# Linear attention and MLP mixer on one core: VectorE subtracts the float32 pairs' maxima, and the tiles stand in three pools

## The chip, the cores and the metric

One NeuronCore of a Trainium2 chip runs the whole program. The metric is the device time of one execution in microseconds (us), the median of the runs. A profile of one execution comes with it: a trace of every instruction on the engines TensorE (PE, its weight loads PEld), VectorE (DVE), ScalarE (ACT), GpSimd (POOL) and the DMA queues, most of them issued from SP.

## The reference

Eight sequences of 576 tokens, eight heads of 64. Attention with an exponential feature map, then a token mixer and a channel mixer:

```python
def phi(x):
    proj = np.einsum('bhsd,df->bhsf', x, w_phi)                      # 128 features
    proj = proj - np.max(np.abs(proj), axis=-1, keepdims=True)
    return np.concatenate([np.exp(proj), np.exp(-proj)], axis=-1)
q_p, k_p = phi(q), phi(k)
kv = np.einsum('bhsf,bhsd->bhfd', k_p, v);  z = np.sum(k_p, axis=2)
x = einsum('bhsf,bhfd->bhsd', q_p, kv) / (einsum('bhsf,bhf->bhs', q_p, z)[..., None] + 1e-06)
# x: heads side by side, [8, 576, 512]
u  = x + (np.maximum(x.T @ w_tok1, 0) @ w_tok2).T                     # tokens 576 -> 256 -> 576
out = u + np.maximum(u @ w_ch1, 0) @ w_ch2                            # channels 512 -> 1536 -> 512
```

The four mixer weights come as 64-bit floats.

## The kernel before

Heads are taken in 32 pairs, four for each batch element. Nearly every product is made of float32r operands split in a high and a low part, three matmuls each (`mm3`, L77 to L82). Pairs 0 to 3 (`i < PLAIN`), the four of batch 0, skip the split: their projections, keys and queries are plain float32. They are what "float32 pairs" means.

Five Python generators are written out in turn by `weave`: `keys` (projection ppk, maximum mxk, exponentials kp, product pkv with v into kv), `queries` (projection ppq and its tail ppt, maximum, difference pm, transposition pt, exponentials qf, split into qh and ql, product pn, division by den into xt), `token_stream` (per batch two halves of 256 channels: px transposes xt, xh and xl are its parts, pa the first product, ah and al the hidden values' parts, ph the second product, added into xt), `load_weights` (24 blocks of the channel weights and seven of the token weights), and `channel_stream` (18 pieces of 256 tokens: uh and ul are the parts of xt, h the up product, gh and gl its parts, acc the down product). A scheduler that simulates the engines' time then sets the order on each engine; each engine takes its instructions in that order, and waits at each for what it needs.

A group of projections is 128 rows by one or two times 128 features, in PSUM. `less_max` takes the absolute maximum over the features on VectorE (L226). In the pairs from 4 on, GpSimd subtracts it (L237) and ScalarE takes the two exponentials, one of each sign (L282). In pairs 0 to 3 GpSimd only negates the maximum (nmx, L229). Keys' exponentials are then four ScalarE instructions of 128 features straight from PSUM, with the maximum or its negative as bias (L285); queries' differences are one ScalarE instruction for each 128 features, with the negative as bias (L235).

A block of weights is converted by ScalarE (L131), four VectorE instructions on the tile `bits` (L132 to L135), and then split by ScalarE (L72) and GpSimd (L75).

Tiles stand in two SBUF pools: `cst` for what stays and `wk` for what turns over. What TensorE streams, and some weights, are made by `streamed`: a tile with 32 spare elements, used from the 16th on. `column` pads the maxima to 32 elements. `eps` takes 40 elements for one.

Of the kernel before, what the change touches and what calls it, by code (L numbers as in the profile page):

```python
# [42 lines left out]
def mixer_kernel(ctx, tc, qk, vm, vt, w_phi, w1, w2, wc1, wc2d, out):  # L43
    nc = tc.nc

    cst = ctx.enter_context(tc.tile_pool(name="cst", bufs=1))
# [8 lines left out]
    def streamed(pool, shape, dtype, **kw):

        n = 1
        for k in shape[1:]:
            n *= k
        t = pool.tile([P, n + 32], dtype, **kw)[:, 16:16 + n]  # L60
        if len(shape) == 3:
            t = t.rearrange("p (a b) -> p a b", a=shape[1])
        return t

    def column(pool, n, **kw):

        return pool.tile([P, 32], F32, **kw)[:, :n]

# [20 lines left out]
    wp2 = streamed(cst, [P, 2, F], F32R, name="wp2")  # L89
    wp = cst.tile([P, F], F32, name="wp")  # L90
# [13 lines left out]
    for j in range(2):  # L104
        t = cst.tile([P, 672], F32, name=f"v{j}")[:, :650].rearrange("p (u j d) -> p u j d", u=5, j=2)
        nc.gpsimd.memset(t[:, 4], 0.0)
        nc.gpsimd.memset(t[:, 0:4, :, D:], 1.0)
        for i in range(2):
            nc.gpsimd.memset(t[i * D:(i + 1) * D, 4, i, D:], 1.0)
# [81 lines left out]
    def less_max(ts, units, name, base=None):  # L191
# [25 lines left out]
        if base is None:  # L217
            part = wk.tile([P, 2, F], F32, tag="part", name=f"part{name}")
            nc.scalar.copy(part[:, :n], ps[:, :n, 1])
# [1 line left out]
            nc.vector.tensor_tensor(pr[:, :n], ps[:, :n, 0], part[:, :n], op=ALU.add)
# [4 lines left out]
        nc.vector.tensor_reduce(mx[:, :n], pr, axis=AX.X, op=ALU.max, apply_absolute_value=True)  # L226
        if base is not None:
            nmx = column(wk, 2, tag="nmx", name=f"nmx{name}")
            nc.gpsimd.tensor_scalar(nmx[:, :n], mx[:, :n], -1.0, None, op0=ALU.mult)  # L229
        if base == D:  # L230
            return pr, nmx, mx
        pm = wk.tile([P, 2, F], F32, tag=f"pm{kind}", name=f"pm{name}", bufs=1 if kind == "t" else 2)
        if base == 0:
            for i in range(n):
                nc.scalar.activation(pm[:, i], pr[:, i], AF.Identity, bias=nmx[:, i:i + 1])  # L235
        else:
            nc.gpsimd.tensor_tensor(pm[:, :n], pr, mx[:, :n].unsqueeze(2).to_broadcast([P, n, F]), op=ALU.subtract)  # L237
        return pm
# [23 lines left out]
    def keys():  # L262
        groups = [[(0, 0), (0, 1)], [(0, 2), (0, 3)], [(1, 0), (1, 1)], [(1, 2), (1, 3)], [None]]
        todo = None
        for i in range(B * NP):
# [11 lines left out]
            for g, us in enumerate(groups):  # L277
                pm = less_max(ts, us, f"k{i}_{g}", plain)
                kp = wk.tile([P, 2, 2, F], F32, tag="kp", name=f"kp{i}_{g}")
                for sg in range(2):  # L280
                    if i >= PLAIN:
                        nc.scalar.activation(kp[:, :len(us), sg], pm[:, :len(us)], AF.Exp, scale=1.0 - 2.0 * sg)  # L282
                        continue
                    for n in range(len(us)):
                        nc.scalar.activation(kp[:, n, sg], pm[0][:, n], AF.Exp, bias=pm[1 + sg][:, n:n + 1],  # L285
                                             scale=1.0 - 2.0 * sg)
# [70 lines left out]
    def turn(i, k, j, pm, tail):  # L357
# [11 lines left out]
        for sg in range(2):  # L369
            full = wk.tile([P, SEG[0][1]], F32, tag="qf", name=f"qf{i}_{k}{j}{sg}")[:, :w]  # L370
# [7 lines left out]
            (nc.gpsimd if sg else nc.vector).tensor_tensor(lo, full, hi.bitcast(F32), op=ALU.subtract)  # L378
# [92 lines left out]
    def channel_mix(i, segs):  # L471
        uh, ul = [], []
        for c in range(NC_):
            h = streamed(wk, [P, CH], F32R, tag=f"uh{c}", name=f"uh{i}_{c}", bufs=1)
# [144 lines left out]
```

## Time and profile before

| | us |
|---|---|
| median of 3 runs | 1182.55 (1182.36 to 1184.48) |
| the profiled execution's own time | 1180.86 |
| its span in the trace | 1178.9 |
| TensorE busy | 1134.0 |
| VectorE busy | 702.9 |
| ScalarE busy | 673.5 |
| GpSimd busy | 584.8 |

A row of the profile's groups reads: line, engine, operation, tiles written and read, shapes, count, then busy us, mean ns of one, idle time of the engine before them and what ended it. The forty slices give busy tenths. Rows by stage give for each stretch the busy us and count of PE, PEld, VectorE, ScalarE and GpSimd, then the clock granted to TensorE, the share of the DMA engines and GB/s. A row of the timeline gives start, duration, engine, line and operation.

### The profile page before, as it was taken

How to read it: one execution, taken by the hardware profiler on the slowest of the kernel's cores; microseconds unless marked ns; L12 is line 12 of the kernel's file. 1: busy time of each engine (PE TensorE's matmuls, PEld its weight loads, DVE VectorE, ACT ScalarE, POOL GpSimd, SP SyncE). 2: the span in 40 equal slices, each digit the busy share in tenths (PEclk: the TensorE clock that was granted, in tenths of full speed). 3: DMA queues.
4: the chain of work that ended last, by engine and by line, in shares of the span. 5: the costliest groups of instructions: out<-in, count | busy, mean ns of one | idle time of the engine just before them, and what ended most of it. 6: DMA issues, size and time to landing. Idle time of an engine off the chain costs nothing.

```text
span 1178.9 us, 24080 instructions
## 1 busy us (share of the span) xinstructions
PE 1134.0 (96%) x9032; PEld 1099.9 (93%) x9032; DVE 702.9 (60%) x1406; ACT 673.5 (57%) x1913; POOL 584.8 (50%) x774
## 2 busy tenths in 40 slices
PE   8877999999999999999999999999999999999998
PEld 6655889998999999998999999999999989999998
DVE  6899783566746666657656565474665666553111
ACT  6988784575746565566646455563665666441110
POOL 3567783465636564565546355462554655430000
PEclk9877799999999999999999999999999999999999
DMA  9543120111101111111111011110111110000000
GB/s 232 177 142 113 31 78 2 49 32 49 31 19 38 42 31 40 41 40 41 31 48 33 19 32 49 31 50 7 43 32 49 40 40 11 19 1 19 19 19 18
DMA packets 65299, 54.30 MB, mean 46 GB/s; under 512 B 44768, under 2 KB 56416, under 8 KB 65184
## 3 DMA queue, kind: packets, MB, share of 16 engines
q1 hardware_dynamic: 63824, 52.41, 15.4%
q8 instruction: 71, 1.16, 0.4%
q10 hardware_dynamic: 1360, 0.36, 0.1%
q14 instruction: 44, 0.36, 0.1%
HBM read 43.32 MB, written 9.44 MB: 45 GB/s over the span
## 4 chain that ended last, share of the span: by engine, by line
PE 84%; DVE 6%; ACT 6%; issue 2%; POOL 1%; DMA 1%; SPq 0%; POOLq 0%; DVEq 0%; ACTq 0%
PE acc L81 26%; PE h L81 26%; PE pkv L308 8%; PE pn L81 7%; PE ph L81 4%; PE pa L81 3%; PE pt L364 2%; PE ppk L212 2%; PE ppq L212 2%; DVE bitsc L135 1%; DVE bitsc L134 1%; PE px L432 1%; DVE bitsc L132 1%; ACT kp L285 1%; DVE den L410 1%
## 5 line engine op out<-in xcount | busy, mean ns | idle before, releaser
L81 PE MATMUL acc<-gh,wc 128*128 128x256 f32 x1728 | 339.7, 283 | 0.1
L81 PEld LDWEIGHTS acc<-gh,wc 128*128 128x128 f32 x1728 | 274.4, 188 | 0.4 <-ACT gh L498 0.4
L81 PE MATMUL h<-ul,wc_h 128*128 128x256 f32 x864 | 245.4, 284 | 1.9 <-POOL ul L479 1.8
L81 PE MATMUL h<-uh,wc_h 128*128 128x256 f32 x864 | 245.7, 285 | 0.5 <-DVE gl L499 0.5
L81 PE MATMUL h<-uh,wc_l 128*128 128x256 f32 x864 | 244.2, 283 | 0.0
L81 PE MATMUL acc<-gl,wc 128*128 128x256 f32 x864 | 243.2, 284 | 0.0
L308 PE MATMUL pkv<-v,kp 128*128 128x65 f32 (+1 forms) x1152 | 166.7, 280 | 6.9 <-ACT kp L285 4.3
L378 POOL TENSOR_TENSOR ql<-qf,qh 128x320 fp32r<-128x320 f32 (+1 forms) x112 | 93.0, 830 | 160.2 <-ACT qh L377 160.0
L308 PEld LDWEIGHTS pkv<-v,kp 128*128 128x128 f32 x1152 | 157.1, 202 | 14.6 <-ACT kp L285 7.9
L81 PEld LDWEIGHTS h<-ul,wc_h 128*128 128x128 f32 x864 | 162.8, 188 | 3.1 <-POOL ul L479 3.1
L81 PEld LDWEIGHTS h<-uh,wc_h 128*128 128x128 f32 x864 | 162.4, 188 | 1.1 <-DVE gl L499 1.1
L81 PEld LDWEIGHTS h<-uh,wc_l 128*128 128x128 f32 x864 | 163.2, 189 | 0.0
L81 PEld LDWEIGHTS acc<-gl,wc 128*128 128x128 f32 x864 | 162.9, 188 | 0.0
L499 DVE SCALAR_TENSOR_TENSOR gl<-h,gh 128x512 fp32r<-128x512 f32 x108 | 74.0, 685 | 144.1 <-ACT gh L498 143.1
L371 ACT ACTIVATE qf<-pt 128x320 f32<-128x320 f32 (+1 forms) x256 | 105.5, 416 | 85.9 <-PE pt L364 84.6
L282 ACT ACTIVATE kp<-pmk 128x256 f32<-128x256 f32 x280 | 96.0, 392 | 72.7 <-POOL pmk L237 69.6
L498 ACT ACTIVATE gh<-h 128x512 fp32r<-128x512 f32 x108 | 64.5, 598 | 112.8 <-PE h L81 112.1
L410 DVE RECIPROCAL den<-den 128x320 f32<-128x320 f32 x64 | 124.7, 1949 | 3.7 <-ACT den L406 2.3
L81 PE MATMUL pn<-qh,kv 128*128 128x320 f32 (+1 forms) x448 | 114.8, 297 | 0.6 <-ACT qh L377 0.3
L378 DVE TENSOR_TENSOR ql<-qf,qh 128x320 fp32r<-128x320 f32 (+1 forms) x112 | 70.1, 626 | 58.1 <-ACT qh L377 57.7
L237 POOL TENSOR_TENSOR pmk<-pk,mxk 128x256 f32<-128x256 f32 (+1 forms) x140 | 86.0, 614 | 35.7 <-DVE mxk L226 35.4
L187 POOL TENSOR_TENSOR stq<-raw,stq 64x512 fp32r<-64x512 f32 (+1 forms) x56 | 80.2, 1433 | 43.5 <-ACT stq L186 36.7
(112 smaller groups left out, 2418.4 us busy)
## 6 DMA issues: line engine op xcount, KB each, us to landing
raw<-in_qk SPq DMA_DIRECT2D x27, 576.0 KB, 3.8
rawc<-in_wc SPq DMA_DIRECT2D x24, 512.0 KB, 3.8
v<-in_vm SPq DMA_DIRECT2D x31, 256.0 KB, 3.4
out_x<-xt SPq DMA_DIRECT2D x12, 256.0 KB, 2.2
out_x<-xt SPq DMA_DIRECT2D x16, 192.0 KB, 2.0
raw<-in_w SPq DMA_DIRECT2D x8, 256.0 KB, 4.1
out_x<-xt SPq DMA_DIRECT2D x16, 128.0 KB, 1.9
pair<-in_qk SPq DMA_DIRECT2D x8, 160.0 KB, 4.5
```

Of the source, the lines that this page charges most:

```text
L81: nc.tensor.matmul(o, a, m, start=first and i == 0, stop=last and i == 2, skip_group_check=group_ok)
L187: nc.gpsimd.tensor_tensor(t[lo:lo + D], src, t[base:base + D].bitcast(F32), op=ALU.subtract)
L212: nc.tensor.matmul(ps[:, i].rearrange("p two f -> p (two f)"), t[:, c:c + P], wp2.rearrange("p two f -> p (two f)"), start=True, stop=True)
L237: nc.gpsimd.tensor_tensor(pm[:, :n], pr, mx[:, :n].unsqueeze(2).to_broadcast([P, n, F]), op=ALU.subtract)
L282: nc.scalar.activation(kp[:, :len(us), sg], pm[:, :len(us)], AF.Exp, scale=1.0 - 2.0 * sg)
L308: nc.tensor.matmul(o, kp[:, n, sg], v, start=g == 0 and n == 0 and sg == 0, stop=u is None, skip_group_check=True)
L364: nc.tensor.transpose(ptr[:, n], r, ident)
L371: nc.scalar.activation(full, src, AF.Exp, scale=1.0 - 2.0 * sg)
L378: (nc.gpsimd if sg else nc.vector).tensor_tensor(lo, full, hi.bitcast(F32), op=ALU.subtract)
L410: nc.vector.reciprocal(den, den)
L498: nc.scalar.activation(gh, ph, AF.Relu)
L499: nc.vector.scalar_tensor_tensor(gl, ph, 0.0, gh.bitcast(F32), op0=ALU.max, op1=ALU.subtract)
```

## The change

In `less_max`, pairs 0 to 3 now do what the others do, with VectorE in GpSimd's place: VectorE subtracts the maxima from the projections in PSUM and writes pm to SBUF, in one instruction for a group of up to 256 columns. The negations go. ScalarE's exponentials of the keys are then one instruction for each sign, from SBUF and without a bias, and the queries' differences are no longer ScalarE's.

```diff
-            pr = pr[:, :n]
+            pr, eng = pr[:, :n], nc.gpsimd
         else:
-            pr = ps[:, :n, 0]
+            pr, eng = ps[:, :n, 0], nc.vector
-        mx = column(wk, 2, tag=f"mx{kind}", name=f"mx{name}")
+        mx = odd.tile([P, 2], F32, tag=f"mx{kind}", name=f"mx{name}")
         nc.vector.tensor_reduce(mx[:, :n], pr, axis=AX.X, op=ALU.max, apply_absolute_value=True)
-        if base is not None:
-            nmx = column(wk, 2, tag="nmx", name=f"nmx{name}")
-            nc.gpsimd.tensor_scalar(nmx[:, :n], mx[:, :n], -1.0, None, op0=ALU.mult)
-        if base == D:
-            return pr, nmx, mx
         pm = wk.tile([P, 2, F], F32, tag=f"pm{kind}", name=f"pm{name}", bufs=1 if kind == "t" else 2)
-        if base == 0:
-            for i in range(n):
-                nc.scalar.activation(pm[:, i], pr[:, i], AF.Identity, bias=nmx[:, i:i + 1])
-        else:
-            nc.gpsimd.tensor_tensor(pm[:, :n], pr, mx[:, :n].unsqueeze(2).to_broadcast([P, n, F]), op=ALU.subtract)
++        eng.tensor_tensor(pm[:, :n], pr, mx[:, :n].unsqueeze(2).to_broadcast([P, n, F]), op=ALU.subtract)
         return pm
...
                 for sg in range(2):
-                    if i >= PLAIN:
-                        nc.scalar.activation(kp[:, :len(us), sg], pm[:, :len(us)], AF.Exp, scale=1.0 - 2.0 * sg)
-                        continue
-                    for n in range(len(us)):
-                        nc.scalar.activation(kp[:, n, sg], pm[0][:, n], AF.Exp, bias=pm[1 + sg][:, n:n + 1],
-                                             scale=1.0 - 2.0 * sg)
+                    nc.scalar.activation(kp[:, :len(us), sg], pm[:, :len(us)], AF.Exp, scale=1.0 - 2.0 * sg)
```

The second part is where tiles stand. `streamed` and `column` go. A pool `st` holds the streamed tiles, without spare elements; a pool `odd` holds v, eps, qf, den and the maxima. Two unused tiles of 32 and 192 bytes stand first in `cst` and `st`:

```diff
+    st = ctx.enter_context(tc.tile_pool(name="st", bufs=2))
+    odd = ctx.enter_context(tc.tile_pool(name="odd", bufs=2))
+    cst.tile([P, 8], F32, name="lead")
+    st.tile([P, 48], F32, tag="lead", name="lead2", bufs=1)
...
-    eps = cst.tile([P, 40], F32, name="eps")[:, :1]
+    eps = odd.tile([P, 1], F32, tag="eps", name="eps", bufs=1)
...
-        t = cst.tile([P, 672], F32, name=f"v{j}")[:, :650].rearrange("p (u j d) -> p u j d", u=5, j=2)
+        t = odd.tile([P, 5, 2, D + 1], F32, tag=f"v{j}", name=f"v{j}", bufs=1)
...
-            h = streamed(wk, [P, CH], F32R, tag=f"uh{c}", name=f"uh{i}_{c}", bufs=1)
+            h = st.tile([P, CH], F32R, tag=f"uh{c}", name=f"uh{i}_{c}", bufs=1)
```

The order on the engines changes up to the 315th instruction of VectorE's 1448 and the 728th of TensorE's 8354; from there on it is the same as before.

VectorE at the program's start, before (mx are the maxima of pair 0's groups, wp_80 the split projection weights, bits a block of weights):

```order
L226 TENSOR_REDUCE mxk_0_114<-ppk_0_111 128x2
L74 CAST wp_80<-wp 128x128
L75 TENSOR_TENSOR wp_80<-wp,wp_80 128x128
L226 TENSOR_REDUCE mxk_1_155<-ppk_1_152 128x2
L226 TENSOR_REDUCE mxq_00_145<-ppq_00_142 128x2
L226 TENSOR_REDUCE mxt_125<-ppt_123 128x1
L132 TENSOR_SCALAR bits_0_134<-bits_0_134 128x512
```

VectorE at the same place in the changed kernel (its lines have other numbers: L218 is the reduction, L220 the subtraction):

```order
L218 TENSOR_REDUCE mxk_0_122<-ppk_0_119 128x2
L66 CAST wp_88<-wp 128x128
L220 TENSOR_TENSOR pmk_0_124<-ppk_0_119,mxk_0_122 128x256
L67 TENSOR_TENSOR wp_88<-wp,wp_88 128x128
L218 TENSOR_REDUCE mxk_1_156<-ppk_1_153 128x2
L220 TENSOR_TENSOR pmk_1_158<-ppk_1_153,mxk_1_156 128x256
L218 TENSOR_REDUCE mxq_00_149<-ppq_00_146 128x2
L220 TENSOR_TENSOR pmq_00_151<-ppq_00_146,mxq_00_149 128x256
```

Each reduction is followed by its subtraction, at once or a few rows on.

VectorE around the low part of the first hidden values of batch 0 (al_0), before (den_1 is pair 3's last reciprocal, bitsc_8 to bitsc_10 are channel weights):

```order
L134 SCALAR_TENSOR_TENSOR bitsc_10_2304<-rawc_10_2302,bitsc_10_2304 128x512
L410 RECIPROCAL den_1_1112<-den_1_1112 128x256
L135 SCALAR_TENSOR_TENSOR bitsc_9_2212<-rawc_9_2210,bitsc_9_2212 128x512
L135 SCALAR_TENSOR_TENSOR bitsc_10_2304<-rawc_10_2302,bitsc_10_2304 128x512
L75 TENSOR_TENSOR xl_0_4_1068<-px_0_4_1064,xh_0_4_1067 128x256
L221 TENSOR_TENSOR pk_4_1194<-ppk_4_1190,partk_4_1192 128x128
L226 TENSOR_REDUCE mxk_4_1196<-pk_4_1194 128x1
L458 SCALAR_TENSOR_TENSOR al_0_1119<-pa_0_962,ah_0_1118 128x512
L221 TENSOR_TENSOR pk_0_1223<-ppk_0_1218,partk_0_1221 128x256
```

VectorE around the same instruction (L436 now) in the changed kernel:

```order
L126 SCALAR_TENSOR_TENSOR bitsc_0_1024_1889<-rawc_0_1024_1887,bitsc_0_1024_1889 128x512
L218 TENSOR_REDUCE mxk_3_1065<-pk_3_1063 128x2
L125 TENSOR_SCALAR bitsc_1_1024_1951<-bitsc_1_1024_1951 128x512
L124 TENSOR_SCALAR bitsc_2_1024_2004<-bitsc_2_1024_2004 128x512
L127 SCALAR_TENSOR_TENSOR bitsc_0_1024_1889<-rawc_0_1024_1887,bitsc_0_1024_1889 128x512
L436 SCALAR_TENSOR_TENSOR al_0_1039<-pa_0_888,ah_0_1038 128x512
L213 TENSOR_TENSOR pk_4_1114<-ppk_4_1110,partk_4_1112 128x128
L126 SCALAR_TENSOR_TENSOR bitsc_1_1024_1951<-rawc_1_1024_1949,bitsc_1_1024_1951 128x512
L125 TENSOR_SCALAR bitsc_2_1024_2004<-bitsc_2_1024_2004 128x512
L218 TENSOR_REDUCE mxk_4_1116<-pk_4_1114 128x1
```

Before, 120 of the conversions' 124 VectorE instructions stand ahead of al_0; now 99 do. The blocks of the last third of wc1 and the last of wc2 have moved behind it.

TensorE around the last matmul of batch 0's token mixing (ph_1_1_1), before (pt and ppk belong to pairs 5 and 6):

```order
L81 MATMUL ph_1_0_1_1538<-w_h,al_1_1452 128x256
L364 MATMUL pt_01_1951<-ident,pmq_01_1869 128x128 x2
L81 MATMUL h_0_1655<-uh_2_1645,wc_h 128x256
L81 MATMUL ph_1_1_1_1577<-w_h,ah_1_1451 128x256
L81 MATMUL ph_1_1_1_1577<-w_l,ah_1_1451 128x256
L81 MATMUL ph_1_1_1_1577<-w_h,al_1_1452 128x256
L308 MATMUL pkv_1882<-v_92,kp_2_1948 128x65 x4
L212 MATMUL ppk_4_2166<-wp_80,stk_1692 128x256
```

TensorE at the same matmul in the changed kernel (pn_11 belongs to pair 4):

```order
L73 MATMUL ph_1_1_1_1497<-w_h,ah_1_1371 128x256
L73 MATMUL ph_1_1_1_1497<-w_l,ah_1_1371 128x256
L73 MATMUL ph_1_1_1_1497<-w_h,al_1_1372 128x256
L204 MATMUL ppq_00_1645<-wp_88,stq_1629 128x256 x2
L73 MATMUL h_0_1575<-uh_2_1565,wc_h 128x256
L73 MATMUL pn_11_1675<-qh_110_1537,kv_4_1181 128x256
L73 MATMUL pn_11_1675<-ql_110_1538,kv_4_1181 128x256
```

Before, the last of these ph matmuls is the 479th on TensorE; now it is the 442nd. The 37 that stood ahead of it and now stand behind belong to pairs 4 to 6.

More of the change, by code (lines that the diff above doesn't have):

```diff
@@ L53, in mixer_kernel @@
     REST = dict(tag="rest", bufs=3)
[L55 to L67, printed above, removed]
     def split(hi, lo, raw, eng_hi, eng_lo):
@@ L86, in mixer_kernel @@
     make_identity(nc, ident)
-    eps = cst.tile([P, 40], F32, name="eps")[:, :1]
+    eps = odd.tile([P, 1], F32, tag="eps", name="eps", bufs=1)
     nc.gpsimd.memset(eps, 1e-6)
-    wp2 = streamed(cst, [P, 2, F], F32R, name="wp2")
+    wp2 = st.tile([P, 2, F], F32R, tag="wp2", name="wp2", bufs=1)
     wp = cst.tile([P, F], F32, name="wp")
@@ L96, in mixer_kernel @@
     w1_l = cst.tile([P, 5, T], F32R, name="w1_l")
-    w2_h = streamed(cst, [P, NT, S], F32R, name="w2_h")
-    w2_l = streamed(cst, [P, NT, S], F32R, name="w2_l")
+    w2_h = st.tile([P, NT, S], F32R, tag="w2_h", name="w2_h", bufs=1)
+    w2_l = st.tile([P, NT, S], F32R, tag="w2_l", name="w2_l", bufs=1)
     wc1_h = cst.tile([P, NC_, E], F32R, name="wc1_h")
@@ L128, in convert @@
         top, low = raw[:, :, 1], raw[:, :, 0]
-        m = streamed(wk, [P, 512], U32, tag="bits", name=f"bits{name}", bufs=3)[:w, :n]
+        m = wk.tile([P, 512], U32, tag="bits", name=f"bits{name}", bufs=3)[:w, :n]
         nc.scalar.activation(m.bitcast(F32), top.bitcast(F32), AF.Abs)
@@ L221, in less_max @@
             nc.vector.tensor_tensor(pr[:, :n], ps[:, :n, 0], part[:, :n], op=ALU.add)
-            pr = pr[:, :n]
+            pr, eng = pr[:, :n], nc.gpsimd
         else:
-            pr = ps[:, :n, 0]
-        mx = column(wk, 2, tag=f"mx{kind}", name=f"mx{name}")
+            pr, eng = ps[:, :n, 0], nc.vector
+        mx = odd.tile([P, 2], F32, tag=f"mx{kind}", name=f"mx{name}")
         nc.vector.tensor_reduce(mx[:, :n], pr, axis=AX.X, op=ALU.max, apply_absolute_value=True)
-        if base is not None:
-            nmx = column(wk, 2, tag="nmx", name=f"nmx{name}")
-            nc.gpsimd.tensor_scalar(nmx[:, :n], mx[:, :n], -1.0, None, op0=ALU.mult)
-        if base == D:
-            return pr, nmx, mx
-        pm = wk.tile([P, 2, F], F32, tag=f"pm{kind}", name=f"pm{name}", bufs=1 if kind == "t" else 2)
-        if base == 0:
-            for i in range(n):
-                nc.scalar.activation(pm[:, i], pr[:, i], AF.Identity, bias=nmx[:, i:i + 1])
-        else:
-            nc.gpsimd.tensor_tensor(pm[:, :n], pr, mx[:, :n].unsqueeze(2).to_broadcast([P, n, F]), op=ALU.subtract)
+        pm = wk.tile([P, 2, F], F32, tag=f"pm{kind}", name=f"pm{name}", bufs=1 if kind == "t" else 2)
+        eng.tensor_tensor(pm[:, :n], pr, mx[:, :n].unsqueeze(2).to_broadcast([P, n, F]), op=ALU.subtract)
         return pm
@@ L369, in turn @@
         for sg in range(2):
-            full = wk.tile([P, SEG[0][1]], F32, tag="qf", name=f"qf{i}_{k}{j}{sg}")[:, :w]
+            full = odd.tile([P, SEG[0][1]], F32, tag="qf", name=f"qf{i}_{k}{j}{sg}")[:, :w]
             nc.scalar.activation(full, src, AF.Exp, scale=1.0 - 2.0 * sg)
@@ L374, in turn @@
                 continue
-            hi = streamed(wk, [P, SEG[0][1]], F32R, tag="qh", name=f"qh{i}_{k}{j}{sg}")[:, :w]
-            lo = streamed(wk, [P, SEG[0][1]], F32R, tag="ql", name=f"ql{i}_{k}{j}{sg}")[:, :w]
+            hi = st.tile([P, 384], F32R, tag="qh", name=f"qh{i}_{k}{j}{sg}")[:, :w]
+            lo = st.tile([P, 384], F32R, tag="ql", name=f"ql{i}_{k}{j}{sg}")[:, :w]
             nc.scalar.activation(hi, src, AF.Exp, scale=1.0 - 2.0 * sg)
@@ L391, in numerators @@
         if j == 0:
-            dens[0] = wk.tile([P, SEG[0][1]], F32, tag="den", name=f"den{i}_{k}", bufs=1)[:, :w]
+            dens[0] = odd.tile([P, SEG[0][1]], F32, tag="den", name=f"den{i}_{k}", bufs=1)[:, :w]
         den = dens[0]
@@ L433, in token_mix @@
             if w < P:
-                xs = streamed(wk, [P, 2, P], F32R, tag="xh", name=f"xs{b}_{h}")
+                xs = st.tile([P, 2, P], F32R, tag="xh", name=f"xs{b}_{h}")
                 nc.scalar.copy(xs[:w], px[:w])
@@ L445, in token_mix @@
                 continue
-            xh = streamed(wk, [P, 2, P], F32R, tag="xh", name=f"xh{b}_{h}_{u}")[:w]
-            xl = streamed(wk, [P, 2, P], F32R, tag="xl", name=f"xl{b}_{h}_{u}")[:w]
+            xh = st.tile([P, 2, P], F32R, tag="xh", name=f"xh{b}_{h}_{u}")[:w]
+            xl = st.tile([P, 2, P], F32R, tag="xl", name=f"xl{b}_{h}_{u}")[:w]
             split(xh, xl, px[:w], nc.scalar, nc.vector)
@@ L473, in channel_mix @@
         for c in range(NC_):
-            h = streamed(wk, [P, CH], F32R, tag=f"uh{c}", name=f"uh{i}_{c}", bufs=1)
-            l = streamed(wk, [P, CH], F32R, tag=f"ul{c}", name=f"ul{i}_{c}", bufs=1)
+            h = st.tile([P, CH], F32R, tag=f"uh{c}", name=f"uh{i}_{c}", bufs=1)
+            l = st.tile([P, CH], F32R, tag=f"ul{c}", name=f"ul{i}_{c}", bufs=1)
             d = 0
@@ L495, in up_proj @@
                     mm3(ph[:, k], (wc1_h[:, c, es], wc1_l[:, c, es]), (uh[c], ul[c]), c == 0, c == NC_ - 1)
-            gh = streamed(wk, [P, 2, CH], F32R, tag="g", name=f"gh{i}_{ep}", bufs=4)
-            gl = streamed(wk, [P, 2, CH], F32R, tag="g", name=f"gl{i}_{ep}", bufs=4)
+            gh = st.tile([P, 2, CH], F32R, tag="g", name=f"gh{i}_{ep}", bufs=4)
+            gl = st.tile([P, 2, CH], F32R, tag="g", name=f"gl{i}_{ep}", bufs=4)
             nc.scalar.activation(gh, ph, AF.Relu)
```

## The prediction

> **What bounds the kernel now.** I read the page's busy table and the forty slices first, then the chain that ended last, then the busy time by stage, then the groups of instructions of the first stages.
>
> ```profile
> PE 1134.0 (96%) x9032; PEld 1099.9 (93%) x9032; DVE 702.9 (60%) x1406; ACT 673.5 (57%) x1913; POOL 584.8 (50%) x774
> PE   8877999999999999999999999999999999999998
> DVE  6899783566746666657656565474665666553111
> ACT  6988784575746565566646455563665666441110
> PEclk9877799999999999999999999999999999999999
> PE 84%; DVE 6%; ACT 6%; issue 2%; POOL 1%; DMA 1%; SPq 0%; POOLq 0%; DVEq 0%; ACTq 0%
> ```
>
> TensorE is full from the sixth slice on, and its clock reaches full speed there. Only the first four or five slices have VectorE and ScalarE as busy as that. The 6% and 6% that they hold of the chain come from there. The stages in numbers (busy us of PE, PEld, DVE, ACT, POOL with counts, then the granted clock, DMA share, GB/s):
>
> ```profile
> 0.00:10.00 10.00, 5.15 (x22) 4.69 (x22) 1.96 (x6) 3.24 (x8) 2.39 (x19) 1.00 0.81 220
> 10.00:42.00 32.00, 31.53 (x136) 25.22 (x138) 27.08 (x55) 27.32 (x81) 15.96 (x23) 0.84 0.81 213
> 42.00:131.00 89.00, 70.09 (x326) 54.16 (x324) 84.19 (x125) 71.80 (x191) 59.19 (x62) 0.76 0.41 124
> 131.00:167.00 36.00, 33.10 (x237) 30.19 (x237) 29.04 (x66) 31.87 (x92) 27.61 (x36) 0.97 0.18 53
> 167.00:191.00 24.00, 24.00 (x206) 24.00 (x206) 12.43 (x24) 14.55 (x40) 13.93 (x17) 1.00 0.13 38
> 191.00:1179.00 988.00, 970.14 (x8117) 961.60 (x8115) 548.23 (x1133) 524.68 (x1504) 465.68 (x620) 1.00 0.11 32
> ```
>
> From 167 us on TensorE is the bound: 206 matmuls in 24.00 us, 116.5 ns each. From 42 to 131 us VectorE is: 84.19 of 89 us busy, 4.8 idle, beside ScalarE's 17.2 idle. The two stages that I cut at 130.6 and 166.4 us end at these VectorE instructions of batch 0's token mixing: the low part of the first half's hidden values (al), and the last of its sums (xt).
>
> ```profile
> 130.55 0.69 DVE L458 SCALAR_TENSOR_TENSOR al<-pa,ah 128x512 fp32r<-128x512 f32 x1 [1.64 <-ACT ah L457]
> 166.38 0.41 DVE L467 TENSOR_TENSOR xt<-ph,xt 128x256 f32<-128x256 f32 x1
> ```
>
> After the second, the channel mixing of batch 0 is free of everything, and TensorE runs full. So the change is worth what it does to these two dates, and to how much TensorE has left behind by then. All instructions that it adds or drops belong to head pairs 0 to 3, which are done by then.
>
> **What is removed and added.**
>
> ```profile
> L285 ACT ACTIVATE kp<-ppk,mxk 128x128 f32<-128x128 f32 x36 | 11.7, 382 | 0.0
> L285 ACT ACTIVATE kp<-ppk,nmxk 128x128 f32<-128x128 f32 x36 | 11.6, 370 | 1.3 <-POOL nmxk L229 1.2
> L235 ACT ACTIVATE pmq<-ppq,nmxq 128x128 f32<-128x128 f32 x32 | 10.4, 381 | 0.8 <-POOL nmxq L229 0.7
> L229 POOL TENSOR_SCALAR nmxk<-mxk 128x2 f32<-128x2 f32 x16 | 6.4, 397 | 6.4 <-DVE wp L74 3.5 <-DVE mxk L226 2.5 <-ACT pmt L235 0.3
> L229 POOL TENSOR_SCALAR nmxq<-mxq 128x2 f32<-128x2 f32 x16 | 6.0, 376 | 14.0 <-DVE mxq L226 9.7 <-ACT kp L285 4.3
> L282 ACT ACTIVATE kp<-pmk 128x256 f32<-128x256 f32 x224 | 81.7, 414 | 66.8 <-POOL pmk L237 63.9 <-PE ppq L212 2.3
> L282 ACT ACTIVATE kp<-pmk 128x128 f32<-128x128 f32 x56 | 14.3, 305 | 5.9 <-POOL pmk L237 5.7
> L221 DVE TENSOR_TENSOR pk<-ppk,partk 128x256 f32<-128x256 f32 x112 | 46.2, 412 | 10.0 <-POOL pmt L237 4.5 <-ACT partk L219 3.3 <-POOL pmk L237 0.9
> L221 DVE TENSOR_TENSOR pk<-ppk,partk 128x128 f32<-128x128 f32 x28 | 7.8, 280 | 0.0
> ```
>
> ScalarE loses 104 instructions of 128 columns (11.7 + 11.6 + 10.4 = 33.7 us) and the four tails, and gains 32 exponentials of 256 columns at 414 ns and 8 of 128 at 305 ns: 15.7 us. It is lighter by 18 us or more. GpSimd loses 40 small negations, 12.4 us for the 32 of two columns. I cost both at nothing: while VectorE is full these two wait for it. VectorE gains 32 subtractions of 256 columns and 8 of 128. The trace has none, but its neighbour L221 also reads one operand from PSUM and one from SBUF: 32 x 0.412 + 8 x 0.280 = 15.4 us.
>
> **The step that moves** is the weights' conversion, four VectorE instructions for each of 24 blocks:
>
> ```profile
> L135 DVE SCALAR_TENSOR_TENSOR bitsc<-rawc,bitsc 128x512 uint32<-128x512 uint32 x24 | 22.7, 950 | 0.2
> L134 DVE SCALAR_TENSOR_TENSOR bitsc<-rawc,bitsc 128x512 uint32<-128x512 uint32 x24 | 21.4, 890 | 0.2
> L132 DVE TENSOR_SCALAR bitsc<-bitsc 128x512 f32<-128x512 f32 x24 | 16.5, 689 | 1.6 <-ACT bitsc L131 1.6
> L133 DVE TENSOR_SCALAR bitsc<-bitsc 128x512 uint32<-128x512 uint32 x24 | 15.3, 639 | 0.2
> ```
>
> That is 75.9 us for 96, 0.79 us each.
>
> Term A, up to al. Counted in the two orders, VectorE has ahead of al 40 subtractions more (+15.4), 21 conversion instructions fewer (-16.6), and one reduction and one addition fewer (-0.8): -2.0 us of work in a stage that VectorE bounds. It is idle there 8.0 us in the first ten, which DMA and the first matmuls set, then 4.9 us between 10 and 42 and 4.8 us after that. The lighter ScalarE may give back some of the 4.9; I take half, -2.4. A is -4.4 us. Its low end takes all of it: -6.9. Its high end gives nothing back and lets every subtraction wait for the reduction just before it, which in the trace moves a start from 0.33 to 0.45 us after the last:
>
> ```profile
> 131.16 0.41 DVE L221 TENSOR_TENSOR pk<-ppk,partk 128x256 f32<-128x256 f32 x1
> 131.61 0.42 DVE L226 TENSOR_REDUCE mxk<-pk 128x2 f32<-128x256 f32 x1
> 160.08 0.41 DVE L221 TENSOR_TENSOR pk<-ppk,partk 128x256 f32<-128x256 f32 x1
> 160.41 0.48 DVE L378 TENSOR_TENSOR ql<-qf,qh 128x320 fp32r<-128x320 f32 x1
> ```
>
> So 40 x 0.12 - 2.0 = +2.8.
>
> Term B, from al to the last xt. VectorE now has 17 conversion instructions more there (+13.4), and pairs 4 to 6 have moved behind: one reciprocal, one low part, eleven of about 0.41 us, -6.9. That is +6.5 us into 36 us with 7.0 idle. Each of the conversions also brings ScalarE and GpSimd work into a stage where they idle 4.1 and 8.4 us, and the maxima, low parts and sums of the token mixing queue behind conversions on VectorE. Between 0 (all of it in the idle time) and +6.5 I take half, +3.3.
>
> Term C. When the last ph matmul issues, TensorE has 37 fewer matmuls behind it than before: those of pairs 4 to 6 come later, when it is full. 37 x 0.1165 = +4.3 us. The cover that hid them, TensorE's own slack before 167 us, is gone. Ends: 0 if TensorE finds as much slack later, and 4.3.
>
> The DMA issues on SP are the same 235 in another order; the weights' blocks now come a little later than the heads' tiles, and 0.41 of the DMA engines' time is used in 42 to 131 us. I cost that at nothing.
>
> Sum: -4.4 + 3.3 + 4.3 = +3.2 us. Against the profiled execution's 1180.9 us that is 1184.1; the median of the runs shown lies 1.7 above it, so 1185.8. The ends of the terms give -6.9 to +13.6.
>
> **The placement.** Worked out from the tiles' sizes, weights start 32 bytes and streamed operands 96 bytes past a multiple of 128 in both kernels; the lead tiles of 32 and 192 bytes see to it. What moves against 128 are v (32 to 0 and 64), the identity (0 to 32), qf and den (32 to 64). Streamed tiles stood 1152 bytes apart, so at four places in 512; now they stand at one.
>
> ```profile
> L81 PE MATMUL h<-uh,wc_h 128*128 128x256 f32 x864 | 245.7, 285 | 0.5 <-DVE gl L499 0.5
> L81 PE MATMUL h<-ul,wc_h 128*128 128x256 f32 x864 | 245.4, 284 | 1.9 <-POOL ul L479 1.8
> L308 PE MATMUL pkv<-v,kp 128*128 128x65 f32 x1024 | 145.0, 279 | 6.9 <-ACT kp L285 4.3 <-ACT kp L282 2.0 <-ACT kv L319 0.3
> L364 PE MATMUL pt<-ident,pmq 128*128 128x128 f32 x256 | 55.9, 284 | 1.4 <-POOL pmq L237 1.4
> ```
>
> Matmuls that read uh and ul, whose tiles alternate between these places, are alike within 1 ns, so the four places are worth nothing. For v and the identity nothing in the trace tells. A tenth of 116.5 ns on those 1280 matmuls would be 15 us, of either sign; I take 0, the value that the four places showed.
>
> **Rivals.**
>
> Faster. VectorE's stage shrinks by all its idle time and by what GpSimd took from it. A conversion's first step cost 689 ns in the mean, and 423 in the two blocks of the same shape that ran early:
>
> ```profile
> L132 DVE TENSOR_SCALAR bits<-bits 128x512 f32<-128x512 f32 x2 | 0.8, 423 | 1.5 <-ACT bits L131 1.5
> L109 POOL MEMSET v<- 64x1 f32 x4 | 0.4, 92 | 0.1
> ```
>
> Something beside it lengthens these steps, and GpSimd's negations took 397 ns for two columns where a fill of one column takes 92. If each negation held VectorE up for 92 ns, 40 of them give 3.7 us back. A is then -6.9 - 3.7 = -10.6, B 0, C 4.3: -6.3, 1176.3. It decides once VectorE's idle time before al falls under 13 us and the conversions behind al fit into the idle 7.0. Against it: GpSimd is itself 77% busy in 131 to 167 us, and the conversions move there.
>
> The Trainium skill ("SBUF — State Buffer", Who interferes with whom) says that VectorE and GpSimd hold a shared port pair exclusively, that a VectorE instruction with two SBUF inputs or in a two-port mode blocks and is blocked, and that one with a single SBUF input is not. By it the new subtractions never wait, and the negations' holding time goes. With the 92 ns above, the sum would be 3.2 - 3.7 = -0.5 us instead, which is the next rival. The rows of the two kinds agree with it in direction; no row measures the holding time.
>
> No change. B fits wholly into the idle time: -4.4 + 0 + 4.3 = -0.1, 1182.4. For it: 7.0 us idle against 6.5 of work. Against it: ScalarE idles only 4.1 there, and the order on each engine is fixed, so not every idle moment can be used.
>
> Much slower, by placement: 1185.8 + 15 = 1201. I give it 0.04, and its mirror 0.02.
>
> **Chances.** A measurement of this kernel can tell 0.2%, 2.4 us. Slower by more: 0.45, nearly all of it the forecast's case, whose own range is 1185 to 1195. Within 0.2%: 0.29. Faster: 0.26. The range takes in the faster rival and the upper end of A to C, short of its last microseconds: 1176 to 1195.
>
> **What the new profile would show.** Right: about 40 VectorE subtractions near 0.41 us, VectorE over 95% busy from 10 us to al, al at about 126 us, conversions still running after it until about 160, the last xt of batch 0 at 163 to 168, and TensorE at 116.5 ns per matmul from there. Wrong, if al comes before 122 (A), if the 36 us from al to xt keep their length (B), if TensorE is full before xt (C), or if pkv or pt matmuls have another pace late in the run (placement).

## The result, and the profile after

The changed kernel takes 1171.66 us (median; 1168.28 to 1174.64) beside 1182.46 for the kernel before on the same chip. The ratio is 0.9912, interval 0.9895 to 0.9929. That is 10.8 us faster, where 1185.8 was forecast, and below the forecast range of 1176 to 1195. Two executions further down, 3326 us in e4_lead80 and 1810 us in f4_d112_e1, ran at a granted clock of 0.33 and 0.56, so the ratios leave them out, and the second, the one traced, has no pace. The changed kernel's own page (busy time by engine, two rows of the forty slices, the chain):

```profile
PE 1116.9 (96%) x9032; PEld 1085.4 (93%) x9032; DVE 711.6 (61%) x1446; ACT 659.0 (56%) x1845; POOL 570.5 (49%) x734
PE   8787789999999999999999999999999999999998
PEclk9788699999999999999999999999999999999999
PE 86%; ACT 6%; DVE 3%; issue 2%; POOL 2%; DMA 1%; SPq 0%; POOLq 0%; ACTq 0%; DVEq 0%
```

TensorE has the same 9032 matmuls and 17 us less busy time. Two places in the changed kernel's timeline, the ones at which the forecast cut the start (now L436 and L445):

```profile
117.20 0.68 DVE L436 SCALAR_TENSOR_TENSOR al<-pa,ah 128x512 fp32r<-128x512 f32 x1
157.15 0.43 DVE L445 TENSOR_TENSOR xt<-ph,xt 128x256 f32<-128x256 f32 x1
```

So al comes 13.4 us earlier and the last xt of batch 0 9.2 us earlier. This looks like the cause, and the experiments will show that it isn't. The busy time by stage (PE, PEld, DVE, ACT, POOL with counts, then clock, DMA share, GB/s), first around the end of the start, then over 900 us of the long stage and over 20 us near its end. Before:

```profile
0.00:97.50 97.50, 82.78 (x369) 64.37 (x369) 81.56 (x141) 78.29 (x220) 53.70 (x84) 0.82 0.64 179
97.50:148.00 50.50, 40.65 (x230) 35.35 (x230) 42.56 (x75) 38.58 (x102) 37.04 (x37) 0.80 0.20 61
148.00:200.00 52.00, 49.44 (x397) 47.54 (x397) 32.24 (x62) 33.17 (x93) 28.34 (x35) 1.00 0.16 46
200.00:1100.00 900.00, 886.20 (x7405) 877.86 (x7404) 533.30 (x1109) 513.03 (x1481) 459.98 (x612) 1.00 0.12 33
1125.00:1145.00 20.00, 20.00 (x172) 20.00 (x171) 3.71 (x6) 3.10 (x7) 2.85 (x4) 1.00 0.08 28
```

After:

```profile
0.00:97.50 97.50, 80.77 (x398) 64.58 (x398) 85.64 (x174) 65.40 (x163) 38.84 (x44) 0.88 0.59 168
97.50:148.00 50.50, 38.95 (x203) 33.33 (x202) 48.23 (x82) 34.67 (x85) 36.30 (x35) 0.76 0.26 82
148.00:200.00 52.00, 48.74 (x392) 47.36 (x391) 31.88 (x61) 34.95 (x97) 30.04 (x37) 0.97 0.16 45
200.00:1100.00 900.00, 885.92 (x7496) 877.77 (x7495) 534.76 (x1114) 515.53 (x1487) 462.50 (x616) 1.00 0.12 34
1125.00:1145.00 20.00, 20.00 (x179) 20.00 (x178) 4.15 (x6) 2.18 (x5) 1.85 (x3) 1.00 0.08 27
```

Read the counts of the first column. At 97.5 us TensorE is 29 matmuls ahead of before, at 148 us 2 ahead (601 to 599), at 200 us 3 behind (993 to 996). The start's lead is gone. Then come 900 us with equal busy time, an equal clock of 1.00, and 91 matmuls more (7496 to 7405, 1.2%). At the end, where only channel mixing is left, it is 179 to 172 in 20 us. The gain is TensorE's pace. One sees it in the timeline too, as the step from one start to the next. Before:

```profile
1130.42 0.28 PE L81 MATMUL acc<-gl,wc 128*128 128x256 f32 x1
1130.54 0.40 PE L81 MATMUL acc<-gh,wc 128*128 128x256 f32 x2
1130.78 0.28 PE L81 MATMUL acc<-gl,wc 128*128 128x256 f32 x1
```

After:

```profile
1130.39 0.28 PE L73 MATMUL acc<-gh,wc 128*128 128x256 f32 x1
1130.51 0.28 PE L73 MATMUL h<-ul,wc_h 128*128 128x256 f32 x1
1130.62 0.28 PE L73 MATMUL h<-uh,wc_l 128*128 128x256 f32 x1
1130.73 0.28 PE L73 MATMUL h<-uh,wc_h 128*128 128x256 f32 x1
```

Three steps take 0.36 us before (one row holds two matmuls), three take 0.34 after. From all starts in the trace I took the step between neighbouring float32r matmuls of 256 columns behind the 1000th, where it is under 130 ns: 5567 of them in the trace of either kernel. I call their mean the pace below:

```
kernel   pace      at 112-115 ns   at 116-119 ns   more
before   117.67      15%             70%            15%
after    115.34      56%             42%             2%
```

Before, the steps spread around 118. After, there are two states, 113 to 114 ns and 117 to 118 ns, with little between. 5567 x 2.33 ns = 13.0 us. The two traced spans differ by 12.4 us, and the changed kernel's 1000th matmul starts 0.7 us later, so nothing is left over. All other steps from there on (other shapes, and waits) add up to 318.8 us before and 318.6 after. The groups' durations, on which the forecast rested, show nearly nothing of it, since their ends are modelled (after, beside 285, 284, 279 and 284 ns before):

```profile
L73 PE MATMUL h<-uh,wc_h 128*128 128x256 f32 x864 | 244.5, 283 | 0.5 <-DVE gl L477 0.5
L73 PE MATMUL h<-ul,wc_h 128*128 128x256 f32 x864 | 243.5, 282 | 1.9 <-POOL ul L457 1.9
L286 PE MATMUL pkv<-v,kp 128*128 128x65 f32 x1024 | 142.8, 276 | 7.3 <-ACT kp L264 7.2
L342 PE MATMUL pt<-ident,pmq 128*128 128x128 f32 x256 | 54.9, 281 | 0.9 <-DVE pmq L220 0.7
```

### The profile page after: what moved, and what is told of

Same layout as the page of the kernel before. It is cut to its first block, busy times and chain, and to the rows that moved or that the text cites. A ratio compares the mean times of both kernels' runs of the same rounds, so it can differ in the third digit from the quotient of the medians.

```text
span 1166.5 us, 23981 instructions
## 1 busy us (share of the span) xinstructions
PE 1116.9 (96%) x9032; PEld 1085.4 (93%) x9032; DVE 711.6 (61%) x1446; ACT 659.0 (56%) x1845; POOL 570.5 (49%) x734
## 3 DMA queue, kind: packets, MB, share of 16 engines
q1 hardware_dynamic: 63824, 52.41, 15.4%
## 4 chain that ended last, share of the span: by engine, by line
PE 86%; ACT 6%; DVE 3%; issue 2%; POOL 2%; DMA 1%; SPq 0%; POOLq 0%; ACTq 0%; DVEq 0%
PE acc L73 26%; PE h L73 25%; PE pkv L286 9%; PE pn L73 7%; PE ph L73 3%; PE pa L73 3%; PE pt L342 3%; PE ppk L204 2%; PE ppq L204 2%; PE pn L376 1%; PE px L410 1%; PE ppk L208 1%; ACT qh L355 1%; ACT qf L349 1%; ACT kp L264 1%
## 5 line engine op out<-in xcount | busy, mean ns | idle before, releaser
L73 PE MATMUL acc<-gh,wc 128*128 128x256 f32 x1728 | 334.5, 281 | 0.2 <-ACT gh L476 0.2
L286 PE MATMUL pkv<-v,kp 128*128 128x65 f32 (+1 forms) x1152 | 164.2, 278 | 7.5 <-ACT kp L264 7.5
L286 PEld LDWEIGHTS pkv<-v,kp 128*128 128x128 f32 x1152 | 154.6, 200 | 12.2 <-ACT kp L264 9.7
L264 ACT ACTIVATE kp<-pmk 128x256 f32<-128x256 f32 (+1 forms) x320 | 109.3, 391 | 82.3 <-POOL pmk L220 74.8
L220 POOL TENSOR_TENSOR pmk<-pk,mxk 128x256 f32<-128x256 f32 (+1 forms) x140 | 86.5, 618 | 36.1 <-DVE mxk L218 30.3
L179 POOL TENSOR_TENSOR stq<-raw,stq 64x512 fp32r<-64x512 f32 (+1 forms) x56 | 80.2, 1433 | 44.8 <-ACT stq L178 35.8
```

The source lines that it names most:

```text
L73: nc.tensor.matmul(o, a, m, start=first and i == 0, stop=last and i == 2, skip_group_check=group_ok)
L179: nc.gpsimd.tensor_tensor(t[lo:lo + D], src, t[base:base + D].bitcast(F32), op=ALU.subtract)
L220: eng.tensor_tensor(pm[:, :n], pr, mx[:, :n].unsqueeze(2).to_broadcast([P, n, F]), op=ALU.subtract)
L286: nc.tensor.matmul(o, kp[:, n, sg], v, start=g == 0 and n == 0 and sg == 0, stop=u is None, skip_group_check=True)
```

## Experiments

Two theories to begin with. **Places**: the changed kernel has four SBUF pools (`cst` and `wk` as before, `st` and `odd` new). By the addresses that the two programs were given, all tiles that TensorE streams past its weights as float32r (the moving operands) now start at one place, 352 mod 512 bytes, and all their weights at 160 mod 512. Before, streamed tiles stood at 96, 224, 352 and 480, and weights at 32, 160, 288 and 416. TensorE's pace follows from that. **Subtraction**: the gain comes from the shorter start.

**The two halves of the change apart.** e1_places has the new pools and the old arithmetic. e2_subs has the old pools and the new arithmetic. Each engine's order of instructions is that of before in the first and that of the changed kernel in the second. In e1_places:

```
+        if base is not None:
+            nmx = odd.tile([P, 2], F32, tag="nmx", name=f"nmx{name}")
+            nc.gpsimd.tensor_scalar(nmx[:, :n], mx[:, :n], -1.0, None, op0=ALU.mult)
+        if base == D:
+            return pr, nmx, mx
...
+                    for n in range(len(us)):
+                        nc.scalar.activation(kp[:, n, sg], pm[0][:, n], AF.Exp, bias=pm[1 + sg][:, n:n + 1],
```

> The three pools and their places as changed; the kept pairs' arithmetic (negated maximum on GpSimd, bias and exp on ScalarE) as before, so that every engine has the instructions of before in the order of before. Theory of places (one start for all streamed tiles shortens the distance of TensorE's 256-column matmuls in the long stage): 1171 to 1175 us, mean start-to-start 115 to 116 ns with a peak near 113, al near 130 us and the last xt of batch 0 near 166 as before. Theory of the subtraction (the gain comes from the start): 1182 us, 117.7 ns, no peak near 113.

> The subtraction on VectorE alone; pools, paddings and places as before; every engine has the order of the changed kernel. Theory of places: al near 117 us and the last xt near 157 us as in the changed kernel, but the matmuls keep 117.7 ns and the time is 1181 to 1185 us (the start's lead is gone by the 1000th matmul). Theory of the subtraction: 1171 to 1173 us. If the earlier start does reach the end: 1173 us at 117.7 ns.

Measured: places alone 1167.55 us, ratio 0.9874 (0.9849 to 0.9899), pace 115.49 ns, al at 132.04 and the last xt at 167.85; the time is 3 us under the expected range. Subtraction alone 1183.37 beside 1182.81, ratio 1.0005 (0.9992 to 1.0018), pace 117.67. Over the long stage, places alone:

```profile
200.00:1100.00 900.00, 885.89 (x7489) 877.73 (x7488) 534.70 (x1114) 515.45 (x1486) 462.37 (x616) 1.00 0.12 33
```

Subtraction alone, with the same 7405 matmuls as before:

```profile
200.00:1100.00 900.00, 886.20 (x7405) 877.84 (x7404) 533.33 (x1109) 513.49 (x1481) 459.97 (x612) 1.00 0.12 33
```

The places make the gain. The subtraction makes the early start (al at 117.15, last xt at 157.17 in e2_subs) and no gain.

**Which of the places.** The changed kernel with 32 elements behind every streamed tile, so that these stand at four places again, while weights, v, identity and query tiles keep their new ones mod 128 (e3_four). And the changed kernel with the streamed pool moved as a whole (e4_lead80):

```
-    t = st.tile([P, n], F32R, **kw)                          # e3_four, for all streamed tiles
+    t = st.tile([P, n + 32], F32R, **kw)[:, :n]
-    st.tile([P, 48], F32, tag="lead", name="lead2", bufs=1)  # e4_lead80
+    st.tile([P, 80], F32, tag="lead", name="lead2", bufs=1)
```

> The changed kernel with 32 elements put behind every tile of the streamed pool, so that its tiles start at four places mod 512 bytes (96, 224, 352, 480) and not one; weights stay at one place, order and arithmetic are those of the changed kernel. Theory of places: the peak near 113 ns goes, mean 117 to 118 ns, 1180 to 1186 us. If the weights' one place (160 mod 512) or the moved v, identity and query tiles make the gain: 1171 us and 115 ns as in the changed kernel.

> The changed kernel with the streamed pool moved on by 128 bytes: all streamed tiles at 480 mod 512, weights at 160. If it counts that all start at one place: 1170 to 1173 us, mean about 115 ns, as in the changed kernel. If it counts how far moving operand and weights lie apart (192 mod 256 in the changed kernel, 64 here; in the kernel before, 64 went with 118.4 ns and 192 with 117.0): mean 117.5 to 118.5 ns, 1183 to 1190 us.

Distance here and below means where the streamed tile starts less where the weights start, in bytes. Measured: four places 1182.27 us, 0.9988 (0.9972 to 1.0004), pace 117.61: the gain is gone. One place at another distance 1181.08 us, 0.9988 (0.9975 to 1.0001), pace 117.21: gone as well, though a little faster than expected. The long stage in e3_four and e4_lead80:

```profile
200.00:1100.00 900.00, 886.15 (x7403) 877.92 (x7402) 532.86 (x1109) 513.33 (x1482) 459.57 (x612) 1.00 0.12 33
```

```profile
200.00:1100.00 900.00, 886.12 (x7428) 877.90 (x7427) 532.70 (x1109) 513.23 (x1482) 460.05 (x612) 1.00 0.12 33
```

One place for all is not enough; which place counts, and the next runs ask whether it is the distance. In the trace of before the moving operand stands at distance 192 mod 256 in 57% of the steps counted for the pace and at 64 in 43%, and e3_four mixes the two as well (46% and 54%). That the identity makes the gain is refuted by e3_four, in which it keeps its new place. v and the query tiles keep theirs there only mod 128, but their share is seen in the traces: steps between matmuls on v of 65 columns add up to 63.3 us before and after, transposes with the identity to 19.0 and 19.1.

**The distance.** Four more lengths of the same lead tile: 112, 128, 32 and 56 elements.

> The changed kernel with its streamed tiles at 96 mod 512 (weights at 160), 448 ahead of the weights where it has 192. If the distance counts mod 256: as the changed kernel, 1168 to 1174 us and mean 115 to 115.6 ns. If it counts mod 512: as yet unknown, up to 1183 us and 117.7 ns.

> The changed kernel with its streamed tiles at 160 mod 512, as the weights: distance 0. By the two distances seen (192: 115.3 ns, 64: 117.2 ns in kernels with one place) 0 lies between; a distance that holds TensorE at 113.3 ns wherever only 256-column matmuls stand would give 1160 to 1165 us, one that holds it at 117.7 ns 1180 to 1184 us; if only being one place and the sign counted, 1171 us.

> The changed kernel with its streamed tiles at 288 mod 512: distance 128 to the weights. Between 64 (117.2 ns, 1181 us) and 192 (115.3 ns, 1171 us): 1171 to 1181 us if the pace goes with the distance evenly; at either end if there is a bound between them.

> The changed kernel with its streamed tiles at 384 mod 512: distance 224, 32 bytes from the changed kernel's 192. If the pace goes smoothly with the distance: 1168 to 1175 us, 115 to 116 ns. If 64-byte lines count: 1178 us or more, since tiles then start in the middle of one.

| streamed tiles behind weights, mod 256 (mod 512) | time, us | ratio, interval | pace, ns |
|---|---|---|---|
| 0 (0), e6 | 1196.34 | 1.0119 (1.0102 to 1.0135) | 119.66 |
| 64 (320), e4 | 1181.08 | 0.9988 (0.9975 to 1.0001) | 117.21 |
| 128 (128), e7 | 1192.14 | 1.0085 (1.0070 to 1.0100) | 118.79 |
| 192 (192), changed kernel | 1171.66 | 0.9912 (0.9895 to 0.9929) | 115.34 |
| 192 (448), e5 | 1174.04 | 0.9927 (0.9906 to 0.9947) | 116.18 |
| 224 (224), e8 | 1187.49 | 1.0052 (1.0035 to 1.0069) | 118.33 |

Between the worst and the changed kernel lie 25 us, with the same instructions in the same order: 5567 x 4.3 ns = 24 us. I had put 0 and 128 between the others; both are slower than any of them. 32 bytes from 192 to 224 cost 16 us; the 64-byte lines of e8's expectation don't explain it, since its tiles at 384 start at a multiple of 64 and the changed kernel's at 352 do not. e5, the same distance mod 256, is like the changed kernel for 900 us and not at the end:

```profile
200.00:1100.00 900.00, 885.88 (x7477) 877.71 (x7476) 533.64 (x1110) 515.28 (x1486) 462.35 (x616) 1.00 0.12 33
1125.00:1145.00 20.00, 20.00 (x172) 20.00 (x171) 3.60 (x6) 3.10 (x7) 2.84 (x4) 1.00 0.08 27
```

172 matmuls in the last 20 us where the changed kernel has 179: here the last stretch stayed at 117.8 ns. It is 863 steps without another shape between them, so the state at its one entry is worth 863 x 4.4 ns = 3.8 us. At distance 0 it is 170, with practically no step under 116 ns in the whole run:

```profile
200.00:1100.00 900.00, 886.43 (x7319) 878.23 (x7317) 530.60 (x1107) 513.21 (x1479) 460.11 (x612) 1.00 0.12 33
1125.00:1145.00 20.00, 20.00 (x170) 20.00 (x168) 3.95 (x8) 2.39 (x4) 0.00 (x0) 1.00 0.10 27
```

**TensorE by itself.** Is the traffic of the other engines needed for that, and what decides between the two states? m1_distances leaves the reference's computation out and runs only matmuls, 27 at a time, between transposes:

```
    for r in range(REPS):
        for d, shift, step in DIST:
            for _ in range(1 + n % 3):
                nc.tensor.transpose(tr, ident, ident)
            run(d, shift, step, RUN, n % 2)
            n += 1
```

> TensorE alone, nothing of the reference computed: runs of 27 float32r matmuls of 256 columns, one to three transposes between runs, 8 runs for each of 25 places of the moving operand against the weights, the other engines idle. Read: mean and spread of the start-to-start distance by place. If the place alone sets the pace: distance 192 near 113 to 116 ns and below 64 (117 to 118), 128 (119) and 0 (119.7); 448 as 192, 320 as 64, 384 as 128; the same with all weights moved by 64 bytes; the alternation of 64 and 192 at 117 to 118. If the other engines' traffic in SBUF is needed for it: all places within 0.5 ns of each other.

Mean step in ns within a run, from its third on, by the number of transposes in front (1, 2 or 3; which of them stands first differs by place). These are the second to fourth of eight passes, and from there the pattern repeats in threes. In the first pass most runs follow each other with no transpose between, because the scheduler drew 38 transposes to the front:

```
distance   three entries         distance   three entries
0          119.8 120   119.8     192        114.1 113.6 117.8
64         117.8 113.3 117.8     224        118.2 118.3 118.2
112        115.0 115.0 116.1     320 (64)   117.8 117.8 117.8
128        118.7 118.6 118.8     384 (128)  118.5 118.8 118.6
176        119.2 119.3 119.3     448 (192)  114   113.3 117.8
weights and operand both moved by 64: 0: 119.3 119.8 119.9   192: 117.8 117.8 113.4
64 and 192 in turn: 116.7 117.8 117.8
```

TensorE alone shows all of it, so no other engine is needed. What counts is the distance mod 256, not the place (320 only stayed at 117.8 where 64 fell to 113.3 at one entry of three). And for 64 and 192 it is a matter of the entry whether a run falls to 113 or stays at 118. The kernel's traces agree. Of the 200 stretches of more than four such steps in the changed kernel, 102 have both states, mostly a few steps at 118 and then 113 to the end, 11 stay at 113 and 87 above it. In e4_lead80 5 have both, 22 stay at 113 and 173 above it.

**Finer steps.** m2_fine: distances 0 to 252 in steps of 4 bytes, three entries each, otherwise as before. At distances 0 to 148 the first entry has no transpose in front, for the same reason.

> TensorE alone, nothing of the reference computed: runs of 27 matmuls of 256 columns as in the run before, but the moving operand's distance to the weights in steps of 4 bytes from 0 to 252, each entered after one, two and three transposes. If 113 ns is a state that a run falls into by the moment at which it is entered, and the place sets which states hold: places around 192 show 113.3 and 117.8 by the entry, others one value whatever the entry (0: 120, 112: 115.0). If a place exists that always holds 113 to 114 ns, it shows here; in the kernel it would be worth up to 5567 x 2 ns = 11 us below 1171.

The mean over the three entries is 118.2 ns at multiples of 16 bytes, and 121.8, 120.6 and 118.7 at 4, 8 and 12 bytes past one. The Trainium skill ("SBUF — State Buffer", Operand start alignment) asks of a float32 operand only a multiple of 4 bytes, and says that this is about legality and that nothing was timed. Here such starts run at up to 123.5 ns. The best place is 112 with means of 114.2 to 115.1 (114.2 to 116.1 with the run before; the 116.9 of a later expectation stands in neither). 192 gave 117.8 at all three entries of this run. The means hide what 112 does. These are the steps of its third entry, from the first one behind the transposes:

```
204 119 116 117 121 119 114 113 113 114 113 113 114 113 113 114 113 113 114 113 ...
```

All eleven runs at 112, eight in m1_distances and three in m2_fine, end at 113.3 ns, after at most 14 steps, whatever stood in front of them. No other place that was tried ended there every time.

**The subtraction's cost, and place 112.** Places alone had come out 4 us below the changed kernel, in different comparisons. So both again on one chip, and both with the streamed tiles at distance 112 (lead tile of 24 elements, each tile 64 elements longer and used from its fifth on).

> The changed kernel once more, beside the next three. 1168 to 1175 us, spread by the stretches that fall into 113 or 118 ns; mean start-to-start 115 to 116 ns.

> The changed places with the arithmetic of before once more. If the subtraction costs nothing (alone it measured +0.05%) and chance made the 4 us: within 0.2% of the changed kernel beside it, both between 1168 and 1173 us. If the forecast's sum holds for the subtraction (+3.2 us, by work that is behind on TensorE): 3 to 4 us below it, 1167 to 1168 us.

> The changed kernel with all streamed tiles 112 bytes mod 256 behind the weights, where TensorE alone took 114.2 to 116.9 ns by the entry (192: 113.3 to 117.8). Theory of entry states: mean 115 to 116 ns, 1168 to 1174 us, and a spread between runs of less than the changed kernel's 0.5%. If starts off 32 bytes cost in the kernel what they do not alone: above 117 ns, 1180 us or more.

> Distance 112 with the arithmetic of before. If the subtraction costs nothing: as the one before it within 0.2%. If it costs 3 us: 3 us below it.

| kernel | time, us | ratio, interval | pace, ns |
|---|---|---|---|
| changed, again | 1168.81 (1166.58 to 1169.89) | 0.9882 (0.9864 to 0.9899) | 115.48 |
| places alone, again | 1171.09 (1165.37 to 1174.71) | 0.9898 (0.9874 to 0.9922) | 115.48 |
| changed, distance 112 | 1170.04 (1167.70 to 1170.34) | 0.9891 (0.9876 to 0.9907) | 115.01 |
| places alone, distance 112 | 1167.15 (1164.03 to 1169.12) | 0.9868 (0.9848 to 0.9888) | none |

The order of the first two has turned round. Over both comparisons the changed kernel has a mean of 1170.0 us in 9 runs (standard deviation 2.4), places alone 1169.2 in 12 (3.3). A cost of 0.7 us is not to be told from 0. At distance 112 the pair comes out as f4's expectation says for a cost of 3 us: the means differ by 2.8 us, give or take 3. So the subtraction costs something between nothing and 3 us, and how much stays open.

Distance 112 has the better pace by 0.5 ns. In its trace, f3_d112, all 92 stretches of 20 steps or more end at 113 ns, after at most 13 steps; in f1_after 46 of the same 92 do. The long stage of f3_d112, then of f1_after:

```profile
200.00:1100.00 900.00, 886.02 (x7508) 877.65 (x7507) 535.52 (x1115) 516.13 (x1486) 463.73 (x616) 1.00 0.12 33
```

```profile
200.00:1100.00 900.00, 885.88 (x7490) 877.72 (x7489) 534.86 (x1113) 515.47 (x1486) 462.11 (x616) 1.00 0.12 33
```

18 matmuls more, about 2 us. But half of the 200 stretches are of 16 steps or fewer, so much of them is spent on the way to 113, and the total shows no gain: the intervals overlap, and no version here is shown to beat the changed kernel. The narrower spread that was expected is there with the subtraction (2.6 us over the runs, 3.3 and 9.3 beside it) and less so without (5.1).

## Why the prediction was wrong, step by step

**The placement** is the step that failed. It said that matmuls on uh and ul "are alike within 1 ns, so the four places are worth nothing". Two errors are in it. The rows' 285 and 284 ns are durations with modelled ends of pipelined instructions; the pace is the step between starts. Within the trace of before, the steps of the up projections do differ by place: 117.2 ns at distance 192 (uh) and 118.8 at 64 (ul). Once all places were at 192, both took 115.3. And a mean over four places in turn can't show what happens when all matmuls have one. The forecast's rival "placement", 15 us of either sign, had the right size and 0.02 for this sign, and was hung on v and the identity. The steps on those did not change (63.3 us, and 19.0 to 19.1). The marks that I named for it, the paces of pkv and pt, were the wrong ones. That the time came out under the range is due to this step alone: with the old places and the new arithmetic it is 1183.37 us, inside the range.

**Term A**, -4.4 us, had the right sign and was mis-sized. With the subtraction alone al moves from 130.55 to 117.15, -13.4, far outside the term's ends of -6.9 and +2.8; the forecast's mark against A, al before 122, was met. VectorE's time up to al, overlaps counted once, falls from 112.8 to 106.3 us, -6.5 where -2.0 was forecast: the 36 subtractions of pairs and 4 of tails start their successors after 0.32 us and cost 12.6, not the 15.4 of their rows (409 and 413 ns in the changed kernel), and the conversions ahead of al fell by 18.0 us, not 16.6. Idle time falls from 17.8 to 10.8, -7.0 where -2.4 was taken. In the channel weights' blocks the conversions' first two steps also became shorter, 0.56 us each instead of 0.61, when GpSimd's negations were gone; that agrees in direction with the rule of the Trainium skill cited in the forecast ("SBUF — State Buffer", Who interferes with whom). The third step, which has two SBUF inputs, became longer, 0.89 instead of 0.83, which does not agree. Moved blocks and their new neighbours are mixed up in both.

**Term B**, +3.3, is right within 1 us: from al to the last xt it is 40.0 us in e2_subs and 35.8 before, +4.2.

**Term C**, +4.3, is too small. It had to give back what A gains, and did. TensorE's 1000th matmul starts at 202.4 us in e2_subs and at 200.7 before; so from the last xt to there C is 1.7 + 13.4 - 4.2 = +10.9, beyond its upper end of 4.3. Single traces carry an error here: in the two of places alone, the same program, the 1000th matmul starts at 202.0 and 207.0 us, with a granted clock of 0.81 and 0.76 between 97.5 and 148 us. From the measured +0.6 us of the whole, C comes to 0.6 + 13.4 - 4.2 = +9.8. The forecast's mark, full TensorE before xt, doesn't occur. The lead is lost between 97.5 and 148 us, where conversions on VectorE now stand between the steps of the token mixing. In e2_subs:

```profile
97.50:148.00 50.50, 37.41 (x201) 31.55 (x202) 48.24 (x82) 34.48 (x85) 35.97 (x35) 0.80 0.27 81
```

```profile
PE ph L81 <- DVE xt L453: 3.4, 2, 2.5
PE pkv L294 <- ACT kp L272: 3.2, 3, 1.3
PE pa L81 <- DVE xl L75: 2.5, 4, 0.9
```

201 matmuls where before there are 230, at the same granted clock of 0.80, VectorE busy for 48.24 of 50.5 us, and TensorE waiting (waits from 97 to 148 us: total us, times, longest) for xt and xl, which queue on VectorE. Before, it waited 1.9 us for xl there, and no wait for xt is among its waits.

The **sum** of the three, +3.2, measured as +0.6 us (-0.9 to +2.1) in e2_subs, +0.7 and +2.8 in the last comparisons. The forecast for this half came out near by luck: A was put 9 us too high and C about 6 us too low, and these nearly cancel. The rivals: "no change" is what the subtraction does alone. "Faster" is what happened, by another mechanism than that rival's.

## What to carry to other kernels

Where TensorE is the bound, read its pace as matmuls per window or as steps between starts, not as the mean duration of a row. Lay the moving operands so that all stand at one distance to the weights modulo 256 bytes, try several distances (of the six tried here 0 is the worst, 112 and 192 the best), and settle this before judging anything else that shifts pools. And date a change of the start by how many matmuls TensorE has started, not by when one tile is ready. At 112 it takes up to 14 steps to reach the fast state, so longer unbroken stretches should gain more there; that was not tried.

## What the runs showed of the hardware

The step between float32r matmuls of 256 columns, each with its own weights, depends on where the moving operand starts against the weights, mod 256 bytes: 113.3 to 120 ns at multiples of 16 bytes, up to 123.5 between them, with all other engines idle at a granted clock of 0.99. At distances 64 and 192 there are two steady states, 113.3 and 117.8 ns, and what ran just before decides between them. At 112 every run settled at 113.3 after at most 14 steps. The Trainium skill ("TensorE: Matmul & The Clock Gate", Back-to-back issue gap) gives N/2.4 + 2.5 ns for a matmul by itself, which makes an estimated 109 ns for 256 columns, and says that in a stream the weight loads set the step too. Nothing measured here came down to 109 on average over a run. What in the memory or the array makes the states wasn't shown. That the next weights are read while the operand streams fits the traces, in which a weight load starts about 3 ns behind each matmul, but no run separated the two reads.
